# Linear attention beside a GELU MLP: permuted Q features, M in 12 slots, denominators inside an output tile

## The chip, the cores and the metric

The kernel runs on one core of a Trainium2 chip. The metric is the device time of one execution in microseconds (us); the time before is the median of six executions.

## What is computed

One normalised input feeds two blocks, and both are added to the input. Everything is bf16 outside; S = 2048 tokens, D = 640 features, 32 heads of 20 features, F = 1536.

```python
xn = layernorm(x)                      # no weights
q, k, v = split(xn @ wqkv)             # 32 heads of 20 features
pq, pk = phi(q), phi(k)                # phi(t) = (t + 1 if t > 0 else exp(t)) + 1e-6
kv  = einsum("bhsd,bhse->bhde", pk, v)
z   = einsum("bhsd->bhd", pk)          # sum over the tokens
num = einsum("bhqd,bhde->bhqe", pq, kv)
den = einsum("bhqd,bhd->bhq", pq, z) + 1e-6
A   = (num / den) @ wo
B   = gelu(xn @ w1 + b1) @ w2 + b2
out = x + A + B
```

There is no softmax, so K and V are reduced over all tokens before any query is used. The kernel goes one step further: the output of the attention block is (pq / den) @ M, where M, of 640 x 640, is the block-diagonal KV of the heads times wo. Dividing by den is a scaling of pq by head and token.

## The kernel before, in words

Tokens lie in 16 tiles of 128, or 4 chunks of 512. Features lie in 5 tiles of 128 partitions. The order of the work on every engine is the order in which the program issues it; a small planner (`Pl.ins`) notes for every named resource who wrote and who read it last, and puts semaphore waits in front of an instruction for each resource in its `reads` and `writes`. A name that stands for more than what an instruction touches gives a wait that the data doesn't need. The PSUM has 8 banks, handed out in a ring (`take`).

In order on TensorE:

1. Layer norm, its transposed copy, and the MLP's first product with GELU on ACT (`h_unit`, L381). All DMAs of weights are issued by SP in this time, Wo in one and W2 in one.
2. K for 16 tiles (L480). `phi` makes PK from it: exp on ACT (L468), then two VectorE instructions (L469, L471).
3. G = xn' PK for 5 feature tiles (`g_group`, L492). Beside it VectorE adds up PK over the tiles (`z_sums`: L501, then L504 fourteen times, in fp32) and splits the sum into a high and a low bf16 half (L506, L507). GpSimd has nothing to do here but one memset (L487).
4. Q for chunk 0 (`q_chunk`, L529): features of the weight are taken with stride 5, so that feature tile j holds features j, j+5, j+10 and so on: each head has 4 features in every tile, one head to 4 partitions.
5. z, transposed onto partitions by one-column matmuls (`z_step`, L512), and spread by a head mask into ZB (L518).
6. K'V (`kvt_step`, L538): wv' G in 5 blocks of 140 or 160 columns, each masked by VectorE (L542) to keep the heads' own products.
7. Q for chunks 1 to 3.
8. M (`m_step`, L554): 5 feature tiles, each of 16 matmuls with 32 columns of weights (2 halves of the output, 2 source tiles, 4 groups of 32 partitions). Each pair of banks is copied to SBUF by one instruction of ACT (L563) or VectorE (L560); all copies name zsum and zhl, whose place M takes, as written.
9. The denominators (`den_all`, L569), 20 matmuls of 32 columns into one bank. VectorE adds 1e-6 (L573) and takes the reciprocal (L575). `spread` copies each head's row to its 4 partitions with 16 DMAs within SBUF (4 on ACT's queue, 12 on SP's), and `scale_pq` multiplies PQ of a chunk by it, one instruction (L579).
10. The output (`out_mm`, L618): 12 matmuls of W2 and 5 of M for each token tile and half of the columns. The W2 part of the first four tiles is issued ahead of their M part. VectorE adds x and b2 (L594) and the result (L629), SP writes it out.

Of the kernel before, what the change touches and what calls it, by code (L numbers as in the profile page):

```python
# [5 lines left out]
ALU = AluOpType  # L6
ACT = mybir.ActivationFunctionType
P = 128
# [104 lines left out]
def bass_parallel_sum__linear_attn_block__dense_activation_gelu__prompt_kernel(  # L113
# [13 lines left out]
    assert DH == 4 * DT and NC == 4 and P == 4 * H and DT * F >= 2 * (DT + 1) * D  # L127
# [4 lines left out]

    e0 = [DH * ((P * t) // DH) for t in range(DT)]
    e1 = [DH * (-((-(P * (t + 1))) // DH)) for t in range(DT)]
    Wd = [e1[t] - e0[t] for t in range(DT)]

    with contextlib.ExitStack() as es:
# [15 lines left out]
        KVT = W1f[:, DT * D:2 * DT * D].rearrange("p (k d) -> p k d", k=DT)  # L153
        Wqkv = sb("Wqkv", [P, DT, 3 * D], BF16)
        W2 = sb("W2", [P, JT, D], BF16)
        Wo = sb("Wo", [P, DT, D], BF16)
# [9 lines left out]
        hmask = sb("hmask", [P, H], BF16)  # L166
        maskKV = [sb(f"maskKV{t}", [P, Wd[t]], BF16) for t in range(DT)]
# [11 lines left out]
        rsp = sb("rsp", [P, NC, CW], BF16)  # L179
# [14 lines left out]
        def bank(b, lo=0, hi=512):  # L194
            return ps[:, b * 512 + lo: b * 512 + hi]
# [15 lines left out]
        r_Wq, r_Wv, r_W2, r_Wo = R_("Wq"), R_("Wv"), R_("W2"), R_("Wo")  # L211
# [12 lines left out]
        r_KVT = R_("KVT")  # L224
        r_M = [R_("M%d" % j) for j in range(DT)]
        r_zsum, r_zhl, r_z, r_ZB = R_("zsum"), R_("zhl"), R_("z"), R_("ZB")
        r_den, r_rden = R_("den"), R_("rden")
        r_rsp = [[R_("rsp%d_%d" % (c, r)) for r in range(4)] for c in range(NC)]
# [12 lines left out]
        def dma(eng, dst, src, writes, reads=()):  # L241
            Pl.ins(eng, lambda e: e.dma_start(dst, src), reads=reads, writes=writes, dma=True)
# [45 lines left out]
        for t in range(DT):  # L288
            band(maskKV[t][:], r_masks, P * t - e0[t], Wd[t] // DH, DH)
        band(hmask[:], r_hmask, 0, H, 4)  # L290
# [164 lines left out]
        dma("sync", Wo[:], A_wo.rearrange("(k p) n -> p k n", p=P), [r_Wo])  # L455
# [31 lines left out]
        Pl.ins(g, lambda e: e.memset(KVT.bitcast(FP32), 0.0), writes=[r_KVT] + r_W1)  # L487
# [11 lines left out]
        def z_sums():  # L499
            a, c = tord[0], tord[1]  # L500
            Pl.ins(v, lambda e: e.tensor_tensor(out=zsum, in0=PK[:, a, :], in1=PK[:, c, :], op=ALU.add),  # L501
                   reads=[r_PK[a], r_PK[c]], writes=[r_zsum])
            for t in tord[2:]:
                Pl.ins(v, lambda e, t=t: e.tensor_tensor(out=zsum, in0=zsum, in1=PK[:, t, :], op=ALU.add),  # L504
                       reads=[r_PK[t], r_zsum], writes=[r_zsum])
            Pl.ins(v, lambda e: e.tensor_copy(zhl[:, 0, :], zsum), reads=[r_zsum], writes=[r_zhl])  # L506
            Pl.ins(v, lambda e: e.tensor_tensor(out=zhl[:, 1, :], in0=zsum, in1=zhl[:, 0, :], op=ALU.subtract),  # L507
                   reads=[r_zsum, r_zhl], writes=[r_zhl])

        def z_step():  # L510
            b = take(1)
            Pl.ins(pe, [(lambda e, j=j, i=i: e.matmul(bank(b, j, j + 1), zhl[:, i, j:D:DT], onesm[:, 0:1],  # L512
                                                      start=(i == 0), stop=(i == 1)))
                        for j in range(DT) for i in range(2)],
                   reads=[r_zhl, r_ones], writes=[B_[b]])
            Pl.ins(v, lambda e: e.tensor_copy(z_sb[:], bank(b, 0, DT)), reads=[B_[b]], writes=[r_z])
            for j in range(DT):
                Pl.ins(v, lambda e, j=j: e.tensor_scalar(ZB[:, j, :], hmask[:], z_sb[:, j:j + 1], None, ALU.mult),  # L518
                       reads=[r_z, r_hmask], writes=[r_ZB])
# [5 lines left out]
        def q_chunk(c):  # L525
            cc = slice(c * CW, (c + 1) * CW)
            for j in range(DT):
                b = take(1)
                Pl.ins(pe, [(lambda e, k=k, j=j, b=b: e.matmul(  # L529
                    bank(b), Wqkv[:, k, j:D:DT], xnT[:, k, cc],  # L530
                    start=(k == 0), stop=(k == DT - 1))) for k in range(DT)],
                    reads=[r_Wq] + sum(r_xnT[c * CH:(c + 1) * CH], []), writes=[B_[b]])
                phi(bank(b), b, 1, PQ[:, j, cc], r_PQ[c][j], [])

        def kvt_step():
            for t in range(DT):
                b = take(1)
                Pl.ins(pe, [(lambda e, k=k, b=b, t=t: e.matmul(  # L538
                    bank(b, 0, Wd[t]), Wqkv[:, k, 2 * D + t * P:2 * D + (t + 1) * P],
                    GTb[:, k, e0[t]:e1[t]], start=(k == 0), stop=(k == DT - 1))) for k in range(DT)],  # L540
                    reads=[r_Wv] + r_GT, writes=[B_[b]])
                Pl.ins(v, lambda e, b=b, t=t: e.tensor_tensor(  # L542
                    out=KVT[:, t, e0[t]:e1[t]], in0=bank(b, 0, Wd[t]), in1=maskKV[t][:], op=ALU.mult),
                    reads=[B_[b], r_masks], writes=[r_KVT])

        def m_step():
            for j in range(DT):
                b = (0, 2, 4, 0, 2)[j]
                fns = []
                for h in range(2):  # L550
                    for i in range(2):
                        for q in range(4):
                            c0 = j + 32 * DT * q
                            fns.append(lambda e, t=q + i, q=q, i=i, h=h, b=b, c0=c0: e.matmul(  # L554
                                bank(b + h, 0, HW)[32 * q:32 * q + 32, :],
                                KVT[:, t, c0:c0 + 31 * DT + 1:DT], Wo[:, t, h * HW:(h + 1) * HW],
                                start=(i == 0), stop=(i == 1)))
                Pl.ins(pe, fns, reads=[r_KVT, r_Wo], writes=B_[b:b + 2])
                if j in (2, 4):
                    Pl.ins(v, lambda e, b=b, j=j: e.tensor_copy(halves(Msb[:, j, :]), pair(b)),  # L560
                           reads=B_[b:b + 2], writes=[r_M[j], r_zsum, r_zhl])
                else:
                    Pl.ins(s_, lambda e, b=b, j=j: e.activation(halves(Msb[:, j, :]), pair(b), ACT.Copy),  # L563
                           reads=B_[b:b + 2], writes=[r_M[j], r_zsum, r_zhl])

        def den_all():
            b = 6
            for j in range(DT):
                Pl.ins(pe, [(lambda e, j=j, c=c: e.matmul(  # L569
                    bank(b)[H * c:H * c + H, :], ZB[:, j, :], PQ[:, j, c * CW:(c + 1) * CW],  # L570
                    start=(j == 0), stop=(j == DT - 1))) for c in range(NC)],
                    reads=[r_ZB] + [r_PQ[c][j] for c in range(NC)], writes=[B_[b]])
            Pl.ins(v, lambda e: e.tensor_single_scalar(den_sb[:], bank(b), 1e-6, ALU.add),  # L573
                   reads=[B_[b]], writes=[r_den])
            Pl.ins(v, lambda e: e.reciprocal(rden[:], den_sb[:]), reads=[r_den], writes=[r_rden])  # L575

        def scale_pq(c):
            cc = slice(c * CW, (c + 1) * CW)
            Pl.ins(v, lambda e: e.tensor_tensor(  # L579
                out=PQ[:, :, cc], in0=PQ[:, :, cc],  # L580
                in1=rsp[:, c:c + 1, :].broadcast_to((P, DT, CW)), op=ALU.mult),
                reads=r_rsp[c] + r_PQ[c], writes=r_PQ[c])

        def spread(c):
            for r in range(4):
                dma(s_ if c == 0 else "sync", rsp[r:P:4, c, :], rden[H * c:H * c + H, :], [r_rsp[c][r]],
                    reads=[r_rden])
# [14 lines left out]
        ring[0] = 3  # L602
# [3 lines left out]
        m_step()  # L606
        den_all()
        for c in range(NC):
            spread(c)
        scale_pq(0)  # L610

        def out_mm(t, lo, hi, b, w0, w1):
            tok = slice(t * P, (t + 1) * P)
            seq = [(HG[:, jb, tok], W2[:, jb, :], [r_HG[t][jb], r_W2]) for jb in range(JT)]
            seq += [(PQ[:, j, tok], Msb[:, j, :], [r_PQ[t // CH][j], r_M[j]]) for j in range(DT)]
            n = len(seq)
            for i in range(lo, hi):
                Pl.ins(pe, [(lambda e, i=i, x=x, bb=bb: e.matmul(  # L618
                    bank(bb, 0, x[1] - x[0]), seq[i][0], seq[i][1][:, x[0]:x[1]],
                    start=(i == 0), stop=(i == n - 1))) for x, bb in zip(w0, w1)],  # L620
                    reads=seq[i][2], writes=[B_[bb] for bb in w1], mark=(i in (JT - 1, n - 1)))
# [12 lines left out]
        ahead = [4, 0, 2, 6]  # L634
        for t, b in enumerate(ahead):
            out_mm(t, 0, JT, b, HALF, [b, b + 1])
# [6 lines left out]
        ring[0] = 4  # L643
# [7 lines left out]
        t = NT - 1  # L651
        xb(t)
# [49 lines left out]
```

## Time and profile before

| | us |
|---|---|
| median of 6 executions | 209.11 |
| lowest, highest | 208.96, 209.68 |
| the profiled execution | 209.25 |
| its span in the profile | 207.5 |
| busy: TensorE matmul | 202.8 |
| busy: VectorE | 108.7 |
| busy: ACT | 73.9 |
| busy: GpSimd (POOL) | 20.1 |
| between 82.0 and 103.6: TensorE busy | 21.55 |
| between 82.0 and 103.6: VectorE busy | 15.24 |
| between 82.0 and 103.6: GpSimd busy | 0.00 |

The span is what the profiler saw of the profiled execution; the rest of its time lies around it. "Busy" of a matmul runs from its start to its modelled end, and neighbours overlap, so the pace of a stream is read from start times or from the chain, not from the mean duration. A few matmul records are missing from the trace, each of which looks like a hole of one matmul.

### The profile page before, as it was taken

The numbers are of one execution on the slowest core, as the hardware profiler recorded it, in microseconds if no ns is written. First come the engines' busy times: TensorE is split into PE (matmuls) and PEld (weight loads), VectorE is DVE, ScalarE is ACT, GpSimd is POOL, SyncE is SP. The second block draws the span as 40 slices with busy tenths as digits, with TensorE's granted clock in tenths as the row PEclk, the third lists the DMA queues.
The fourth block names the chain that finished last, engine by engine and source line by source line (L and its number), as shares of the span: only waits on it lengthen the run. The fifth ranks groups of instructions, "written<-read, shape, count | busy, mean of one in ns | idle before, by whom it ended". The sixth has DMA issues, their size and how long they took to land.

```text
span 207.5 us, 3961 instructions
## 1 busy us (share of the span) xinstructions
PE 202.8 (98%) x1616; PEld 140.8 (68%) x1622; DVE 108.7 (52%) x213; ACT 73.9 (36%) x146; POOL 20.1 (10%) x57
## 2 busy tenths in 40 slices
PE   7899999999999999999999999999999999999995
PEld 2799887444457777777757556677777777777775
DVE  4788692000008888998068888823853322523322
ACT  2799887666676445111153556100000000000000
POOL 2245447500020000000000000000000000000000
PEclk9999999999999999999999999999999999999999
DMA  5997975999000000000000002941111110010002
GB/s 157 350 279 108 211 108 100 342 319 361 21 0 0 3 0 0 3 0 0 3 0 0 0 2 46 377 140 51 63 66 37 60 35 32 32 35 32 32 33 65
DMA packets 23371, 18.16 MB, mean 88 GB/s; under 512 B 9912, under 2 KB 23352, under 8 KB 23352
## 3 DMA queue, kind: packets, MB, share of 16 engines
q1 hardware_dynamic: 23136, 17.77, 30.5%
q8 instruction: 13, 0.21, 0.4%
q10 hardware_dynamic: 216, 0.13, 0.3%
q14 instruction: 6, 0.05, 0.1%
HBM read 12.62 MB, written 2.62 MB: 73 GB/s over the span
## 4 chain that ended last, share of the span: by engine, by line
PE 96%; DVE 1%; DMA 1%; issue 0%
PE ps L618 36%; PE ps L381 25%; PE ps L492 10%; PE ps L480 10%; PE ps L529 10%; PE ps L554 1%; DMA xPK<-in_A_x_dram 1%; DVE stats L326 1%; PE ps L538 1%; PE ps L569 1%; PE ps L313 0%; PE ps L512 0%; PE ps L298 0%; DVE xn_tm L354 0%; DVE W L659 0%
## 5 line engine op out<-in xcount | busy, mean ns | idle before, releaser
L618 PE MATMUL ps<-W,HG 128*128 128x320 bf16 (+2 forms) x396 | 54.6, 295 | 0.0
L381 PE MATMUL ps<-xnT,W 128*128 128x128 bf16 (+2 forms) x477 | 52.9, 272 | 0.2
L618 PEld LDWEIGHTS ps<-W,HG 128*128 128x128 bf16 x396 | 38.1, 98 | 14.6 <-issue 0.4
L381 PEld LDWEIGHTS ps<-xnT,W 128*128 128x128 bf16 x480 | 36.9, 98 | 15.8 <-issue 0.3
L385 ACT ACTIVATE HG<-ps,b1c 128x128 bf16<-128x128 f32 (+2 forms) x96 | 41.5, 475 | 12.3 <-PE ps L381 10.7
L629 DVE TENSOR_TENSOR W<-ps,xnT 128x640 bf16<-128x640 f32 x15 | 12.4, 825 | 36.9 <-PE ps L618 36.5
L469 DVE TENSOR_SCALAR ek<-ek 128x512 bf16<-128x512 bf16 (+1 forms) x36 | 10.9, 303 | 38.0 <-ACT ek L468 36.8
L468 ACT ACTIVATE ek<-ps 128x512 bf16<-128x512 f32 (+1 forms) x36 | 23.2, 645 | 20.7 <-PE ps L529 11.0
L618 PE MATMUL ps<-Msb,PQ 128*128 128x320 bf16 (+2 forms) x165 | 24.2, 295 | 0.0
L480 PE MATMUL ps<-Wqkv,xnT 128*128 128x320 bf16 x160 | 21.9, 299 | 0.0
L492 PE MATMUL ps<-xPK,xn_tm 128*128 128x320 bf16 x160 | 21.9, 299 | 0.0
L529 PE MATMUL ps<-xnT,Wqkv 128*128 128x512 bf16 x97 | 21.4, 379 | 0.2
L618 PEld LDWEIGHTS ps<-Msb,PQ 128*128 128x128 bf16 x165 | 15.9, 98 | 5.9
L480 PEld LDWEIGHTS ps<-Wqkv,xnT 128*128 128x128 bf16 x160 | 15.7, 98 | 6.2
L492 PEld LDWEIGHTS ps<-xPK,xn_tm 128*128 128x128 bf16 x160 | 15.7, 98 | 6.1
L529 PEld LDWEIGHTS ps<-xnT,Wqkv 128*128 128x128 bf16 x100 | 11.7, 118 | 9.5
L326 DVE BATCH_NORM_STATS2 stats<-xPK 128x6 f32<-128x320 bf16 x32 | 15.1, 473 | 3.8 <-DMA xPK<-in_A_x_dram 3.3
L471 DVE SCALAR_TENSOR_TENSOR PQ<-ps,ek 128x512 bf16<-128x512 f32 x20 | 13.8, 691 | 2.1
L471 DVE SCALAR_TENSOR_TENSOR xPK<-ps,ek 128x640 bf16<-128x640 f32 x16 | 13.2, 825 | 1.7
L504 DVE TENSOR_TENSOR Msb<-Msb,xPK 128x640 f32<-128x640 f32 x14 | 11.6, 825 | 0.5
L496 ACT ACTIVATE W<-ps 128x640 bf16<-128x640 f32 x5 | 3.5, 704 | 18.2 <-PE ps L492 18.2
L354 DVE TENSOR_SCALAR xn_tm<-xPK,aggr,rstd 128x640 bf16<-128x640 bf16 (+2 forms) x17 | 7.3, 434 | 2.7 <-POOL rstd L342 1.5
(57 smaller groups left out, 76.5 us busy)
## 6 DMA issues: line engine op xcount, KB each, us to landing
xnT<-in_A_x_dram SPq DMA_DIRECT2D x4, 640.0 KB, 6.4
Wqkv<-in_A_wqkv_dram SPq DMA_DIRECT2D x3, 800.0 KB, 6.7
out_dram<-W SPq DMA_DIRECT2D x15, 160.0 KB, 1.8
W<-in_B_w_dram SPq DMA_DIRECT2D x4, 480.0 KB, 5.9
W<-in_B_w_dram SPq DMA_DIRECT2D x1, 1920.0 KB, 16.1
xPK<-in_A_x_dram SPq DMA_DIRECT2D x2, 640.0 KB, 7.0
Wo<-in_A_wo_dram SPq DMA_DIRECT2D x1, 800.0 KB, 10.5
xPK<-in_A_x_dram SPq DMA_DIRECT2D x4, 160.0 KB, 3.8
```

Source lines behind the costliest of these rows:

```text
L326: Pl.ins(v, lambda e: e.bn_stats(stats[:, s, 6 * h:6 * h + 6], x_in[:, t, h * HW:(h + 1) * HW]), reads=r_x[t], writes=[r_stats[s]])
L381: Pl.ins(pe, [(lambda e, k=k: e.matmul(bank(b, 0, w), W1[:, k, jb * P:(jb + 1) * P], xnT[:, k, tok], start=(k == 0), stop=(k == DT - 1))) ...
L385: Pl.ins(s_, lambda e: e.activation(HG[:, jb, tok], bank(b, 0, w), ACT.Gelu_apprx_tanh, bias=b1c[:, jb:jb + 1]), reads=[B_[b], r_b1c], wri ...
L468: Pl.ins(s_, lambda e: e.activation(e2, src, ACT.Exp), reads=br, writes=[r_ek[s]])
L469: Pl.ins(v, lambda e: e.tensor_scalar(et, et, 1.0, 1e-6, ALU.min, ALU.add), reads=[r_ek[s]], writes=[r_ek[s]])
L471: Pl.ins(v, lambda e: e.scalar_tensor_tensor(out=d2, in0=src, scalar=0.0, in1=e2, op0=ALU.max, op1=ALU.add), reads=br + [r_ek[s]], writes= ...
L480: fns.append(lambda e, k=k, h=h, b=b, t=t: e.matmul(bank(b + h, 0, HW), xnT[:, k, t * P:(t + 1) * P], Wqkv[:, k, D + h * HW:D + (h + 1) * ...
L492: Pl.ins(pe, [(lambda e, t=t, h=h, b=b, f=f, i=i: e.matmul(bank(b + h, 0, HW), xn_tm[:, t, f * P:(f + 1) * P], PK[:, t, h * HW:(h + 1) * H ...
L504: Pl.ins(v, lambda e, t=t: e.tensor_tensor(out=zsum, in0=zsum, in1=PK[:, t, :], op=ALU.add), reads=[r_PK[t], r_zsum], writes=[r_zsum])
L529: Pl.ins(pe, [(lambda e, k=k, j=j, b=b: e.matmul(bank(b), Wqkv[:, k, j:D:DT], xnT[:, k, cc], start=(k == 0), stop=(k == DT - 1))) for k in ...
L618: Pl.ins(pe, [(lambda e, i=i, x=x, bb=bb: e.matmul(bank(bb, 0, x[1] - x[0]), seq[i][0], seq[i][1][:, x[0]:x[1]], start=(i == 0), stop=(i = ...
L629: Pl.ins(v, lambda e: e.tensor_tensor(out=halves(out_sb[:, s, :]), in0=pair(b), in1=halves(x_res[:, t, :]), op=ALU.add), reads=B_[b:b + 2] ...
```

## The change

The order of Q's features is changed. Of a head's 20 features, 8 go to feature tile 0 or 1 (heads 0 to 15) or to tile 2 or 3 (heads 16 to 31) in each of the two, and 4 to tile 4. The columns of wq are copied into that order by 25 GpSimd instructions, into the place of wk, once K is done; the sum z and K'V are put in the same order. Then:

- Wo is loaded as 8 overlapping slots of 128 rows, one for each 4 heads, and K'V is computed in 8 blocks of 80 columns into two banks, masked by three VectorE instructions and split into three pieces (KVP) by four GpSimd copies.
- For feature tiles 0 to 3 of M, 4 matmuls give one half of the output; for tile 4 it is 8: 48 in all.
- Each bank of M is copied by itself, the left half of the columns by ACT and the right half by VectorE, and each has its own name in the planner; zsum and zhl are no longer named as written.
- The order around M is: the left half of tile 0's W2 product, the denominators in the other bank of that pair, M (with the addition of 1e-6 after its second feature tile), the reciprocal and the spreads, the right half of tile 0's W2 product, and tiles 1 to 3.
- A spread is three DMAs of 128 rows for each chunk, all on ACT's queue, with a repeated source; the scaling of a chunk is three instructions.

```diff
-        Wo = sb("Wo", [P, DT, D], BF16)
+        Wo = sb("Wo", [P, NW, D], BF16)
...
-        dma("sync", Wo[:], A_wo.rearrange("(k p) n -> p k n", p=P), [r_Wo])
+        for w in range(NW):
+            dma("sync", Wo[:, w, :], A_wo[E0[w]:E0[w] + P, :], [r_Wo[w]])
...
-        Pl.ins(g, lambda e: e.memset(KVT.bitcast(FP32), 0.0), writes=[r_KVT] + r_W1)
+        def parts(ap, i):
+            v4 = ap.rearrange("p (h t) -> p h t", t=DH)
+            if i == DT - 1:
+                return v4[:, :, 2 * TA:DH]
+            return v4[:, HH * (i // 2):HH * (i // 2) + HH, TA * (i % 2):TA * (i % 2) + TA]
+
+        def plain(ap, i):
+            return ap[:, i * P:(i + 1) * P].rearrange("p (h t) -> p h t", t=TB if i == DT - 1 else TA)
+
+        Pl.ins(g, lambda e: e.memset(KVP[2], 0.0), writes=[r_KVP[2]] + r_W1)
+        for k in range(DT):
+            for i in range(DT):
+                Pl.ins(g, lambda e, k=k, i=i: e.tensor_copy(plain(Wqkv[:, k, D:2 * D], i), parts(Wqkv[:, k, 0:D], i)),
+                       reads=[r_Wq], writes=[r_Wk, r_WqP])
...
-            Pl.ins(v, lambda e: e.tensor_copy(zhl[:, 0, :], zsum), reads=[r_zsum], writes=[r_zhl])
...
+            for i in range(DT):
+                Pl.ins(v, lambda e, i=i: e.tensor_copy(plain(zhl[:, 0, :], i), parts(zsum, i)),
+                       reads=[r_zsum], writes=[r_zhl])
...
-                    bank(b), Wqkv[:, k, j:D:DT], xnT[:, k, cc],
+                    bank(b), Wqkv[:, k, D + j * P:D + (j + 1) * P], xnT[:, k, cc],
                     start=(k == 0), stop=(k == DT - 1))) for k in range(DT)],
-                    reads=[r_Wq] + sum(r_xnT[c * CH:(c + 1) * CH], []), writes=[B_[b]])
+                    reads=[r_WqP] + sum(r_xnT[c * CH:(c + 1) * CH], []), writes=[B_[b]])
...
+                Pl.ins(pe, [(lambda e, k=k, b=b, w=w: e.matmul(
+                    bank(b, (w % 4) * WD, (w % 4) * WD + WD), Wqkv[:, k, 2 * D + E0[w]:2 * D + E0[w] + P],
+                    GTb[:, k, w * WD:(w + 1) * WD], start=(k == 0), stop=(k == DT - 1)))
+                    for w in ws for k in range(DT)],
                     reads=[r_Wv] + r_GT, writes=[B_[b]])
...
+        def m_copy(j, b, h):
+            cols = slice(h * HW, (h + 1) * HW)
+            if h == 0:
+                Pl.ins(s_, lambda e: e.activation(Msb[:, j, cols], bank(b + h, 0, HW), ACT.Copy),
+                       reads=[B_[b + h]], writes=[r_M[j][h]])
+            else:
+                Pl.ins(v, lambda e: e.tensor_copy(Msb[:, j, cols], bank(b + h, 0, HW)),
+                       reads=[B_[b + h]], writes=[r_M[j][h]])
+
+        def m_step(js, bs, after):
+            for n, (j, b) in enumerate(zip(js, bs)):
                 for h in range(2):
-                    for i in range(2):
+                    fns, reads = [], []
+                    for a in range(2 if j == DT - 1 else 1):
                         for q in range(4):
...
+                    Pl.ins(pe, fns, reads=reads, writes=[B_[b + h]])
+                    m_copy(j, b, h)
+                if n == 1:
+                    after()
...
-            for r in range(4):
-                dma(s_ if c == 0 else "sync", rsp[r:P:4, c, :], rden[H * c:H * c + H, :], [r_rsp[c][r]],
+            for r, (h, n) in enumerate(((0, HH), (HH, HH), (0, H))):
+                src = rdv[H * c + h:H * c + h + n].broadcast_to((n, P // n, CW))
+                dma(s_, rsp[:, c, r, :], src, [r_rsp[c][r]] + (sum(r_xn, []) if c + r == 0 else []),
                     reads=[r_rden])
...
-        ahead = [4, 0, 2, 6]
-        for t, b in enumerate(ahead):
+        out_mm(0, 0, JT, b0, HALF[:1], [b0])
+        den_mm(b0 + 1)
+        m_step([0, 1, DT - 1, 2, 3], ahead[1:] + ahead[1:3], lambda: den_eps(b0 + 1))
+        den_rec()
+        for c in range(NC):
+            spread(c)
+        scale_pq(0)
+        out_mm(0, 0, JT, b0, HALF[1:], [b0 + 1])
+        for t in range(1, 4):
+            b = ahead[t]
             out_mm(t, 0, JT, b, HALF, [b, b + 1])
```

## The prediction

> **What bounds the kernel now.** I read the page first: busy shares, then the chain that ended last.
>
> ```profile
> PE 202.8 (98%) x1616; PEld 140.8 (68%) x1622; DVE 108.7 (52%) x213; ACT 73.9 (36%) x146; POOL 20.1 (10%) x57
> ...
> PE 96%; DVE 1%; DMA 1%; issue 0%
> ```
>
> TensorE is the chain for 96% of the span, at full clock in all 40 slices. So only two things count: matmul time taken out of its stream, and holes that other engines put into it. The chain in order of time, around the change:
>
> ```profile
> 99.88 3.67 PE ps L492 x27
> 103.55 0.05 issue
> 103.60 5.34 PE ps L529 x24
> 108.94 0.36 PE ps L512 x10
> 109.31 1.58 PE ps L538 x25
> ...
> 127.08 3.03 PE ps L554 x80
> 130.11 1.08 PE ps L569 x20
> 131.19 3.91 PE ps L618 x28
> ```
>
> Columns: start, length, what. L538 is K'V, L554 is M, L569 the denominators, L618 the output products. There is no hole at 103.6 (a record of one 0.216 us matmul is missing there), and from M to the first W2 product TensorE spends 131.19 - 127.08 = 4.11 us. Then the waits, and the other engines on the timeline:
>
> ```profile
> PEld ps L554 <- ACT Msb L563: 0.3, 1, 0.3
> DVE PQ L579 <- DMA rsp<-rden: 4.6, 1, 4.6
> ```
> ```profile
> 83.76 0.81 DVE L501 TENSOR_TENSOR Msb<-xPK 128x640 f32<-128x640 bf16 x1
> 84.61 12.00 DVE L504 TENSOR_TENSOR Msb<-Msb,xPK 128x640 f32<-128x640 f32 x14
> 96.65 0.49 DVE L506 CAST Msb<-Msb 128x640 bf16<-128x640 f32 x1
> 97.17 0.83 DVE L507 TENSOR_TENSOR Msb<-Msb 128x640 bf16<-128x640 f32 x1
> ...
> 131.13 0.82 DVE L560 CAST Msb<-ps 128x640 bf16<-128x640 f32 x1 [0.90 <-ACT Msb L563]
> 131.87 0.68 DVE L573 TENSOR_SCALAR den_sb<-ps 128x512 f32<-128x512 f32 x1
> 132.59 3.35 DVE L575 RECIPROCAL rden<-den_sb 128x512 bf16<-128x512 f32 x1
> 140.54 1.49 DVE L579 TENSOR_TENSOR PQ<-PQ,rsp 128x2560 bf16<-128x2560 bf16 x1 [4.60 <-DMA rsp<-rden]
> ```
>
> M waits once for its own copies. The reciprocal, spread and scaling end at 142.0; TensorE first needs scaled PQ at 144.2, so they have 2.1 us to spare.
>
> **What the Trainium skill says.**
> 1. "SBUF — State Buffer", Who interferes with whom: GpSimd's SBUF ports are VectorE's second pair, taken as an exclusive lock; a VectorE instruction with two SBUF inputs, or in a two-port mode, and a GpSimd instruction that reads SBUF block each other. The trace has one such overlap and agrees. A VectorE normalisation ran from 32.91 to 33.36:
>
> ```profile
> 33.03 0.53 POOL L280 TENSOR_SCALAR_AFFINE_SELECT maskKV<-maskKV 128x140 bf16<-128x140 bf16 x1
> 33.64 0.34 POOL L284 TENSOR_SCALAR_AFFINE_SELECT maskKV<-maskKV 128x140 bf16<-128x140 bf16 x1
> ...
> 38.57 0.42 POOL L280 TENSOR_SCALAR_AFFINE_SELECT hmask<-hmask 128x32 bf16<-128x32 bf16 x1
> ```
>
> The select beside it took 0.53 us, the same one alone 0.34: 0.19 longer, so it got the port about 0.13 us before VectorE's recorded end.
> 2. "TensorEngine Tiling (Array Packing)", Key Properties: changing the tiling mode drains TensorE. The trace agrees: the start times of single matmuls leave 0.09 us extra before the first 32-column matmul and 0.10 after the last.
> 3. "TensorE: Matmul & The Clock Gate", Back-to-back issue gap: columns / 2.4 + 2.5 ns. The trace's 140-column matmuls come every 60 to 61 ns, as that gives.
>
> **The change, part by part.**
>
> *M.* Before: 80 matmuls of 32 columns, in 20 groups of four that start together, 0.136 us apart: 2.72, plus 0.15 waiting for a bank and 2 x 0.03 of group starts, 2.93 us. Denominators 5 x 0.216 = 1.08, drain 0.10: 4.11, as the chain says. After: 48 matmuls, 12 groups, 1.63 + 0.03. With 1.08 and 0.10: 2.85. **Gain 1.27.** The 12 W2 matmuls of tile 0's first half only move ahead of it (12 x 0.136 = 1.63 either way); the number of mode changes stays. They also cover the last phi of chunk 3, which ends at 128.92, while the denominators' last group now starts near 129.6.
>
> *The denominator bank.* Tile 0's second half writes the bank in which the denominators stood, so it now waits for the addition of 1e-6 (VectorE), queued behind two M copies. With chunk 3's matmuls over at 126.92: W2 half to 128.55, drain to 128.64, denominators to 129.72, M to 131.38. A copy sees its product 0.35 us after the group's start (ACT started 0.35 after j=0's last group). A half copy costs: VectorE 0.82 - 320 x 1.09 ns = 0.47 (slope from 0.82 at 640 and 0.68 at 512), next one 0.08 sooner as its rows show; ACT 0.70 - 320 x 0.83 ns = 0.43. VectorE: copies at 130.24 and 130.64, addition 131.04 to 131.72, seen at 131.77. TensorE would be ready at 131.49. **Stall 0.3** (0 to 0.7). By the same sums the M products that reuse a bank find it free: j=2 at 130.84 against 130.54, j=3 at 131.11 against about 131.05. The copies no longer wait for each other through the zsum/zhl names (the 0.90 wait shown); before, that cost only VectorE.
>
> *K'V.* 25 matmuls took 1.58. After: 40 of 80 columns. Price 80/2.4 + 2.5 = 36 ns; the one-column matmuls of L512 with full weight loads came 40 ns apart, so 36 to 40: 1.44 to 1.60. Value -0.05; if a weight load bound at 56 ns, the pace of 128-column matmuls, +0.66. Its masks (three VectorE instructions of about 1.1 us, not five of 1.95) come earlier. The four small GpSimd copies into KVP follow by 117 at the latest; M needs them at 129.7.
>
> *Permuted Q weights.* 25 GpSimd copies of 128x128, after the last K matmul (82.0) and before chunk 0 of Q (103.6): they write where Wk lay, and chunk 0 waits for all 25. Nothing in the trace shows a GpSimd copy. Bounds: not below the 128x128 memset's 0.205, not above the select with 32 short rows, 0.42; I take 0.30 (the 128x128 select took 0.29), plus 0.07 hand-over between dependent GpSimd instructions. Free of VectorE: 25 x 0.37 = 9.3, done at 91.3. But zsum runs from 83.76 with two SBUF inputs each. Four copies before it; then copy and sum alternate at 0.70 (0.83 less the 0.13 above) + 0.30 = 1.0: 15 sums to 98.8, 19 copies done; the other six alternate with the short zhl pieces at about 0.5: 101.8. **Cost 0, with 1.8 us to spare.** The zhl pieces (ten instead of two, about 3.1 us instead of 1.35) also end some 5 us later than 98, near 103; the first phi needs VectorE at 105.3 and z at 108.8. The Q matmuls keep 512 columns at 0.216.
>
> *Reciprocal, spread, scaling.* VectorE does three more half copies after the addition (0.40 apart), so the reciprocal starts at about 133.0 and ends 136.3; 13 wait instructions at 0.06 each (SP's pace) stand ahead of the first spread; three DMAs of 128 rows instead of four of 32, issued at 0.6 each, landing 1.9 to 2.6 after issue: 141. Scaling in three pieces (0.69 + 0.69 + 0.42, from 1.49 for 2560), the first ones while the last lands: 141.5. TensorE needs it at 131.8 + 7 x 12 x 0.136 = 143.2. **Hidden, 1.7 us to spare.** All 12 spreads move from SP to ACT, behind which nothing waits; SP's outputs lose their queue-mates. The later scalings cost VectorE 0.3 more each, at 40% load. Eight Wo DMAs instead of one delay W2's issue by some 3 us to 41; it landed in 16 and is needed at 126.9.
>
> *Sum.* -1.27 + 0.3 - 0.05 = -1.0. The profiled execution took 209.25 with a span of 207.5; so 208.2 and 206.5. It lies 0.14 above the median of 209.11: **208.1**.
>
> **Rivals.**
> A. *The forecast*, 207.8 to 208.5.
> B. *The full saving without the bank stall*: VectorE's addition is early enough. 209.1 - 1.3 = 207.75.
> C. *Copies bind M.* VectorE's five half copies and the addition are 2.7 us of work beside 1.66 of M; if each is slower by 0.15, TensorE waits about 0.7 more: 208.8. For: M's copies are halves with a fixed part each. Against: three bank pairs.
> D. *GpSimd is late at 103.6: slower.* Place: chunk 0's first matmul. Price: the lateness, one for one. It decides when 25 copies take more than 103.6 + 1.0 + 0.4 - 82.0 = 23 us, 0.92 each. With 0.45 a copy: 3 before zsum, 15 beside it at 1.15 to 101.0, 7 at 0.65 to 105.6: 2.0 late, 210.1. Shut out entirely until zhl ends at 99.9: 21 x 0.37 more, 107.7, 4.1 late, 212.2. For: zsum keeps the port 80% of 14 us. Against: the lock passes on at each instruction's end, and the estimate has 1.8 us left.
> E. *The spread is late.* 128-row DMAs with a repeated source are not in the trace. Over 1.7 us late it costs TensorE the rest: 208.5 to 209.5.
>
> **Chances.** A 0.44, B 0.08, C 0.13 (half of it under 208.7), D 0.27 (0.04 still faster, 0.06 about even, 0.17 slower), E 0.08 (0.02 faster, 0.02 even, 0.04 slower). About 0.2% (0.42 us) is what a measurement of this kernel can tell from no change. Faster by more than that: 0.44 + 0.08 + 0.06 + 0.04 + 0.02 = 0.64; within it 0.07 + 0.06 + 0.02 = 0.15; slower 0.17 + 0.04 = 0.21. The range goes from just under B, 207.6, to 209.9: some 0.11 of D lies above it, little below. The likeliest case's own range is A's.
>
> **What would show it.** Right: the row of M with 48 matmuls in about 1.7 us; TensorE's wait for the addition of 1e-6 near 131.5 of 0.2 to 0.4; no wait of the first Q matmul on GpSimd; GpSimd's last Wqkv copy ending by 103. Wrong: a wait of TensorE on GpSimd at 103.6 (D), waits on ACT's or VectorE's M copies between 130 and 133 (C), or on VectorE's PQ scaling at 143 (E); K'V at over 2 us.

## The result, and the profile after

| | before | after |
|---|---|---|
| median, us | 209.62 (208.95 to 211.43, 58 runs) | 208.39 (207.82 to 210.3, 27 runs) |
| ratio, 95% interval | 1 | 0.9936 (0.9918 to 0.9954) |
| profiled execution, us | 209.25 | 208.84 |
| its span | 207.5 | 207.1 |
| first recorded matmul of Q's chunk 0 to the start of VectorE's last instruction, us | 101.67 | 100.42 |

The change makes the kernel faster by 0.64% (0.46 to 0.82%); the medians differ by 1.23 us. 208.1 and a change of 1.0 had been forecast. The median of before, 209.11 in six runs, was 209.62 in 58: single executions of one kernel lie up to 2.5 us apart. In the traces of the kernels below, Q's chunk 0 begins anywhere between 103.4 and 105.4 (but for the kernel with 50 copies, which holds it back), though nothing ahead of it on TensorE was changed. So the traces are compared by the last row of the table, which leaves that part out: in it the gain is 1.25 us. (The very first matmul of chunk 0 has no record in either trace, nor in most of those below; the row counts from the second.)

The page of the kernel after, with the group of GpSimd copies that is new in it (busy time, mean ns, idle time before it):

```profile
PE 201.7 (97%) x1599; PEld 137.5 (66%) x1605; DVE 111.6 (54%) x230; ACT 73.7 (36%) x148; POOL 34.0 (16%) x83
...
L509 POOL COPY Wqkv<-Wqkv 128x128 bf16<-128x128 bf16 x25 | 15.1, 603 | 22.9 <-PE ps L490 21.4
```

GpSimd has 14 us more to do, and the end of the program doesn't see it. The chain in order of time (start, length, what; L539 is z, L566 K'V, L610 M, L620 the denominators, L673 the output products, and its first row here is tile 0's left half):

```profile
104.11 5.34 PE ps L556 x24
109.45 0.23 PE ps L539 x10
109.68 1.46 PE ps L566 x40
...
127.33 1.63 PE ps L673 x12
128.96 1.19 PE ps L620 x20
130.15 0.30 PE ps L610 x8
...
130.47 0.89 DVE Msb L595 x2
131.36 0.61 DVE den_sb L626
...
132.02 72.49 PE ps L673 x549
...
204.53 0.29 DVE W L722
```

The last row of the chain of before is

```profile
205.27 0.29 DVE W L659
```

The terms are best read from start times, because a piece of the chain can begin at the modelled end of a matmul or at the start of the next one. TensorE's rows of before in the timeline (start, length, engine and line, count):

```profile
108.78 0.52 PE L512 MATMUL ps<-onesm,Msb 128*128 128x1 bf16 x10
109.17 1.72 PE L538 MATMUL ps<-W,Wqkv 128*128 128x140 bf16 x25
110.94 16.14 PE L529 MATMUL ps<-xnT,Wqkv 128*128 128x512 bf16 x73
...
131.12 13.21 PE L618 MATMUL ps<-W,HG 128*128 128x320 bf16 x96
```

From the first z matmul to chunk 1 of Q it is 110.94 - 108.78 = 2.16 before and 111.19 - 109.29 = 1.90 after (rows below): -0.26 for z and K'V, of which the chain gives 0.13 to z (0.36 to 0.23) and 0.12 to K'V (1.58 to 1.46). From there to the W2 product that follows M and the denominators it is 131.12 - 110.94 = 20.18 before; after, less the 1.63 us of W2 that only moved ahead, 132.02 - 111.19 - 1.63 = 19.20: -0.98. Together -1.24, where the stretch gave -1.25. Ahead of the rows above, at 20.98, the chain has a hole of 0.45 us, long before any changed instruction of TensorE. The trace of before has none there; more on it below.

The chain leaves TensorE at 130.45 and comes back at 132.02 through two copies of M and the addition of 1e-6: that is the one new wait. TensorE's own rows and VectorE's, from the timeline of after (in brackets the idle time before and what ended it):

```profile
85.12 12.00 DVE L527 TENSOR_TENSOR Msb<-Msb,xPK 128x640 f32<-128x640 f32 x14
...
109.29 0.39 PE L539 MATMUL ps<-onesm,Msb 128*128 128x1 bf16 x10
...
111.19 16.14 PE L556 MATMUL ps<-xnT,Wqkv 128*128 128x512 bf16 x73
127.16 1.79 PE L673 MATMUL ps<-W,HG 128*128 128x320 bf16 x12
...
129.97 1.80 PE L610 MATMUL ps<-Wo,W 128*32 128x320 bf16 x48
132.02 11.58 PE L673 MATMUL ps<-W,HG 128*128 128x320 bf16 x84 [0.24 <-DVE den_sb L626]
143.44 5.60 PE L673 MATMUL ps<-Msb,PQ 128*128 128x320 bf16 x40
...
131.28 0.68 DVE L626 TENSOR_SCALAR den_sb<-ps 128x512 f32<-128x512 f32 x1
...
141.03 1.03 DVE L635 TENSOR_TENSOR PQ<-PQ,xn_tm 128x1024 bf16<-128x1024 bf16 x2 [0.78 <-DMA xn_tm<-rden]
```

M is 48 matmuls in 1.8 us (80 in 3.1 before), and TensorE waits for the addition: 0.24 us after the modelled end of M, 0.31 by start times (worked out below). The reciprocal ran from 133.07 for 3.34 us; the last row is the end of the scaling of chunk 0, done at 142.06, 1.4 us before the first product of PQ and M.

### The profile page after: what moved, and what is told of

It reads as the page before. It is cut to its first block, busy times and chain, and to the rows that moved or that the text cites. A ratio compares the mean times of both kernels' runs of the same rounds, so it can differ in the third digit from the quotient of the medians.

```text
span 207.1 us, 3983 instructions
## 1 busy us (share of the span) xinstructions
PE 201.7 (97%) x1599; PEld 137.5 (66%) x1605; DVE 111.6 (54%) x230; ACT 73.7 (36%) x148; POOL 34.0 (16%) x83
## 3 DMA queue, kind: packets, MB, share of 16 engines
q10 hardware_dynamic: 1752, 1.58, 4.4%
## 4 chain that ended last, share of the span: by engine, by line
PE 95%; DVE 2%; DMA 1%; issue 1%
PE ps L673 36%; PE ps L390 25%; PE ps L515 10%; PE ps L490 10%; PE ps L556 10%; DMA xPK<-in_A_x_dram 1%; DVE stats L335 1%; PE ps L566 1%; PE ps L620 1%; DVE Msb L595 0%; PE ps L322 0%; DVE den_sb L626 0%; PE ps L307 0%; PE ps L610 0%; DVE W L722 0%
## 5 line engine op out<-in xcount | busy, mean ns | idle before, releaser
L673 PE MATMUL ps<-W,HG 128*128 128x320 bf16 (+2 forms) x396 | 54.8, 295 | 0.2 <-DVE den_sb L626 0.2
L673 PEld LDWEIGHTS ps<-W,HG 128*128 128x128 bf16 x396 | 38.1, 98 | 14.8 <-DVE den_sb L626 0.5
L673 PE MATMUL ps<-Msb,PQ 128*128 128x320 bf16 (+2 forms) x165 | 24.2, 295 | 0.0
L673 PEld LDWEIGHTS ps<-Msb,PQ 128*128 128x128 bf16 x165 | 15.9, 98 | 5.9
L509 POOL COPY Wqkv<-Wqkv 128x128 bf16<-128x128 bf16 x25 | 15.1, 603 | 22.9 <-PE ps L490 21.4
L556 PEld LDWEIGHTS ps<-xnT,Wqkv 128*128 128x128 bf16 x100 | 9.7, 98 | 11.4
```

Source lines behind the costliest of these rows:

```text
L509: Pl.ins(g, lambda e, k=k, i=i: e.tensor_copy(plain(Wqkv[:, k, D:2 * D], i), parts(Wqkv[:, k, 0:D], i)), reads=[r_Wq], writes=[r_Wk, r_WqP])
L556: Pl.ins(pe, [(lambda e, k=k, j=j, b=b: e.matmul(bank(b), Wqkv[:, k, D + j * P:D + (j + 1) * P], xnT[:, k, cc], start=(k == 0), stop=(k == ...
L673: Pl.ins(pe, [(lambda e, i=i, x=x, bb=bb: e.matmul(bank(bb, 0, x[1] - x[0]), seq[i][0], seq[i][1][:, x[0]:x[1]], start=(i == 0), stop=(i = ...
```

## The experiments

In the table the last column is the stretch from the first recorded matmul of Q's chunk 0 to the start of VectorE's last instruction, in the profiled execution of each. Each ratio is to executions of before made beside that kernel, whose medians were 209.62, 209.75 and 209.72. Unless said otherwise, a kernel is an edit of the kernel after.

| kernel | median us (range, runs) | ratio to before, 95% | stretch, us |
|---|---|---|---|
| before | 209.62 (208.95 to 211.43, 58) | 1 | 101.67 |
| after | 208.39 (207.82 to 210.3, 27) | 0.9936 (0.9918 to 0.9954) | 100.42 |
| the same again | 208.46 (207.85 to 210.3, 22) | 0.9942 (0.9918 to 0.9966) | 100.42 |
| W2 half split | 208.09 (207.85 to 209.59, 7) | 0.9935 (0.9900 to 0.9970) | 100.11 |
| false waits back | 209.67 (209.15 to 211.54, 14) | 1.0003 (0.9978 to 1.0028) | 101.64 |
| M twice | 209.45 (209.19 to 211.76, 22) | 0.9995 (0.9970 to 1.0019) | 101.75 |
| M copied by pairs | 209.09 (208.24 to 211.59, 20) | 0.9983 (0.9958 to 1.0007) | 100.69 |
| order of before | 209.15 (208.74 to 211.29, 20) | 0.9970 (0.9945 to 0.9995) | 101.30 |
| before, without its false waits | 209.57 (208.88 to 211.25, 20) | 1.0001 (0.9976 to 1.0026) | 101.49 |
| 50 copies on GpSimd | 215.59 (214.35 to 216.12, 4) | 1.0252 (1.0195 to 1.0309) | not used |
| few sums | 208.64 (one run) | one run only | not used |

### The kernel after, once more

No edit: it shows how far the stretch can be trusted.

> The changed kernel once more, beside the kernels that it is compared with. Theory (TensorE's stream got shorter by eight groups of M, z and K'V, and a new wait of 0.3 us for the addition of 1e-6 gives some of it back): 1.2 to 1.3 us under the kernel before. Rival (the saving is scatter of the start, where this kernel's profile has a hole of 0.45 us and the other has none): within 0.4 us of the kernel before.

The median came again within 0.1 us, and the stretch was 100.42 both times, in an execution whose chunk 0 began 0.1 us later. So differences of 0.1 us in the stretch are read here, on the strength of this one repetition; in the medians, with 20 runs each, the interval is 0.5 us wide to either side.

### M's products doubled: what is a group of M worth on TensorE?

```diff
-                    Pl.ins(pe, fns, reads=reads, writes=[B_[b + h]])
+                    Pl.ins(pe, fns + fns, reads=reads, writes=[B_[b + h]])
```

The second pass computes the same values over again.

> Every matmul of M is issued twice (the second overwrites or repeats the first; tile 4 of M comes out the same), so M has 24 groups of four instead of 12, with the same copies. Theory (M is paid one for one in TensorE's stream, 0.136 us a group): 12 x 0.136 = 1.63 us more, less the 0.3 of the wait for the addition, which the longer M hides: 1.3 us slower than the changed kernel. Rival (the copies bind M): under 0.5 us slower.

The chain of it:

```profile
129.48 3.26 PE ps L610 x96
132.74 72.43 PE ps L673 x549
```

The stretch grew by 1.33. 96 products took exactly twice the 1.63 us of 12 groups, without a wait among them, and the wait for the addition is gone from the chain, since TensorE now comes 1.6 us later: 1.63 - 0.31 = 1.32 was due, 1.33 came. A group of M costs TensorE 0.136 us one for one. The copies have twice as long for each bank here; that they keep up at the full pace is seen in the kernel after, whose 48 products run without a wait.

### The wait for the addition taken out: three W2 products held back

```diff
-        out_mm(0, 0, JT, b0, HALF[:1], [b0])
+        out_mm(0, 0, 9, b0, HALF[:1], [b0])
         den_mm(b0 + 1)
...
         scale_pq(0)
+        out_mm(0, 9, JT, b0, HALF[:1], [b0])
         out_mm(0, 0, JT, b0, HALF[1:], [b0 + 1])
```

Three of the 12 W2 products (0.41 us) come after M instead of ahead of the denominators; they fill the wait.

> Only the place of three of tile 0's left W2 matmuls changes: nine stand ahead of the denominators, three after M. Theory: they fill the 0.31 us in which TensorE waits for the addition of 1e-6, and the last phi (done 0.2 us ahead of need) still comes in time; TensorE has no idle time between M and W2 but the drain of 0.1, and the time falls by 0.3 us against the changed kernel. Rival (the wait is not for the addition but for M's last copies or the change of the tiling mode): the hole stays, 0 us.

TensorE goes from M straight to W2; in the chain there is no detour over VectorE. The stretch is shorter by 0.31. The same is read from start times: M's last group and the W2 product behind it, first in after, then in this kernel:

```profile
131.47 0.31 PE L610 MATMUL ps<-Wo,W 128*32 128x320 bf16 x4
132.02 0.31 PE L673 MATMUL ps<-W,HG 128*128 128x320 bf16 x1 [0.24 <-DVE den_sb L626]
```
```profile
130.92 0.31 PE L610 MATMUL ps<-Wo,W 128*32 128x320 bf16 x4
131.16 0.31 PE L673 MATMUL ps<-W,HG 128*128 128x320 bf16 x1
```

0.55 us from one to the other with the wait, 0.24 without: 0.31. The change of the tiling mode is in both, so it is not the cause. The bank stall was real and cost what the forecast gave for it, and rival B (no stall) was wrong for the kernel as it was changed. In the medians it gives 208.09 against 208.39, which the runs can't tell apart; by the trace it is the best version found here.

### The false waits put back

```diff
-                       reads=[B_[b + h]], writes=[r_M[j][h]])
+                       reads=[B_[b + h]], writes=[r_M[j][h], r_zsum, r_zhl])
```

In both branches of the copy: each copy of half of M names zsum and zhl again, so it waits for the one before it on the other engine.

> The changed kernel with zsum and zhl named again as written by every copy of M, so that ten half copies on two engines go one after the other. Theory: 0.5 us each in a row, so the addition of 1e-6 ends at 133.0 and not 132.0, and TensorE's second half of tile 0 starts 1.0 us later: 0.8 to 1.5 us slower than the changed kernel. Rival (as in the kernel before, such waits cost VectorE alone): 0 us.

The timeline of it, the last group of M and the W2 products behind it (M's first group was at 131.28):

```profile
133.85 0.32 PE L610 MATMUL ps<-Wo,W 128*32 128x320 bf16 x4 [0.28 <-DVE Msb L595]
134.45 11.68 PE L673 MATMUL ps<-W,HG 128*128 128x320 bf16 x84 [0.28 <-DVE den_sb L626]
```

and its waits, the two engines for each other (us in all, times, longest):

```profile
DVE Msb L595 <- ACT Msb L592: 3.7, 4, 1.8
ACT Msb L592 <- DVE Msb L595: 2.1, 3, 0.7
```

The stretch is 1.22 longer, nearly the whole gain of the change: ACT and VectorE take turns instead of working side by side, so M's banks and the addition come too late. (Its chunk 0 began 1.3 us later, which the stretch leaves out. That was lost before 13.5 us, where no changed instruction stands: the first 15 matmuls of the MLP took 1.60 us there and 1.00 in after.)

### The same edit the other way, in the kernel before

```diff
-                           reads=B_[b:b + 2], writes=[r_M[j], r_zsum, r_zhl])
+                           reads=B_[b:b + 2], writes=[r_M[j]])
```

> The kernel before, without zsum and zhl as written by the copies of M; nothing else. Theory: VectorE's addition and reciprocal start 0.5 us earlier, in front of slack of 2.1 us: no change of the time (within 0.1 us). Rival (the false waits are part of what the change gained): 0.3 us or more faster than the kernel before.

M's row in the timeline of the kernel before:

```profile
127.01 3.10 PE L554 MATMUL ps<-Wo,W 128*32 128x320 bf16 x80
```

and without the false waits:

```profile
126.96 2.92 PE L554 MATMUL ps<-Wo,W 128*32 128x320 bf16 x80
```

The stretch is 0.18 shorter, more than the 0.1 expected, and M's row shows all of it: 2.92 for 3.10. ACT's second copy had waited for its first one through a name (0.80 us from start to start; the two took 1.50 together, and 1.30 without the false wait), and held the banks that the last feature tile of M was to write. By the traces, removing the false waits alone was worth 0.2 us in the old arrangement; the medians, 209.57 and 209.72, can't tell. They cost 1.2 in the new one. The likely reason is that M now fills its banks in 1.63 us, not 2.92, through twice as many copies; no run tries these two apart.

### M copied by whole pairs, one engine each

```diff
-                    m_copy(j, b, h)
+                m_pair(n, j, b)
```

`m_pair` copies both halves with one instruction, ACT for the even and VectorE for the odd ones, as before the change.

> The changed kernel, but M is copied by pairs of banks, tile by tile, one instruction of ACT or VectorE in turn, as in the kernel before, without false waits. Theory: VectorE's copy of the second tile takes 0.82 instead of two halves of 0.40, so the addition of 1e-6 ends 0.25 us later and TensorE's wait grows from 0.3 to 0.55: 0.2 to 0.3 us slower than the changed kernel. Rival (copies bind M): 0.7 us or more slower.

The detour in its chain, as it stood at 130.47 in that of after (L603 is VectorE's copy, L634 the addition; the last Q matmul ended at 127.11):

```profile
130.60 0.82 DVE Msb L603
131.42 0.61 DVE den_sb L634
```

The stretch is 0.27 longer. The detour over VectorE explains it. VectorE's first copy can start only when both halves of a pair are there, 3.49 us after the last Q matmul (130.60 - 127.11) instead of 3.14 (130.47 - 127.33), and it is one of 0.82 us with the addition queued behind it. So the addition begins 4.23 us after the last Q matmul, and in after 3.95 (131.28 - 127.33): 0.28 later, the whole difference. Copying by halves is worth some 0.3 us. (The medians differ by 0.7, which their interval of 0.5 to either side does not set apart from 0.3.)

### M and the denominators in the old order, in banks of their own

```diff
-        out_mm(0, 0, JT, b0, HALF[:1], [b0])
-        den_mm(b0 + 1)
-        m_step([0, 1, DT - 1, 2, 3], ahead[1:] + ahead[1:3], lambda: den_eps(b0 + 1))
+        ahead = [(b0 + d) % 8 for d in (4, 0, 2, 6)]
+        m_step([0, 1, DT - 1, 2, 3], [b0, (b0 + 2) % 8, (b0 + 4) % 8, b0, (b0 + 2) % 8], lambda: None)
+        den_mm((b0 + 7) % 8)
+        den_eps((b0 + 7) % 8)
...
-        out_mm(0, 0, JT, b0, HALF[1:], [b0 + 1])
-        for t in range(1, 4):
+        for t in range(4):
```

All W2 products come after, so nothing stands between chunk 3 of Q and M.

> The changed kernel, but M stands straight after Q's chunk 3, then the denominators, then all W2 products, as in the kernel before. Theory: M's right halves can be copied only when VectorE is through with the last phi, 2.0 us after Q's last matmul, so the two tiles that reuse a bank wait, and Q's end to W2's start takes 4.4 us instead of 3.1: 1.3 us slower than the changed kernel, about the kernel before. Rival (twelve slots alone bring the saving, the order brings nothing): within 0.3 us of the changed kernel.

The timeline, the last 12 matmuls of M and VectorE:

```profile
129.39 0.72 PE L610 MATMUL ps<-Wo,W 128*32 128x320 bf16 x12 [0.80 <-DVE Msb L595]
...
128.24 0.69 DVE L481 SCALAR_TENSOR_TENSOR PQ<-ps,ek 128x512 bf16<-128x512 f32 x1
128.85 2.07 DVE L595 CAST Msb<-ps 128x320 bf16<-128x320 f32 x5
```

The stretch is 0.88 longer, where 1.3 was expected: the size was missed, because VectorE made its five copies back to back, 0.40 apart, once it was free. The place is as thought. VectorE is busy with the last phi of chunk 3 and starts its first copy at 128.85; before that it can't empty a bank of M, so TensorE waits 0.80 us in the middle; M began at 127.11 and the W2 products at 131.12, 4.01 us later, where the kernel before took 4.11. With the order of before, most of what 32 fewer matmuls save would be lost again in that wait; the 1.63 us of W2 products ahead of M are what hides the phi.

### Twice the copies on GpSimd: where does the cover end?

```diff
-                Pl.ins(g, ...)
+                for _ in range(2):
+                    Pl.ins(g, ...)
```

Each of the 25 copies of wq is issued twice.

> The changed kernel with each of the 25 GpSimd copies of the Q weights made twice. Theory (a copy takes 0.36 with its hand-over alone and 0.86 beside a zsum addition, and chunk 0 waits for the last): 5 to 84.4, 15 beside zsum to 97.4, 30 alone to 108.1; TensorE waits 4.0 us at 104.1: 3.5 to 4.5 us slower than the changed kernel, and VectorE's sums take 12.0 us as before. Rival (no copy bound the start of chunk 0, or VectorE loses the time): under 1 us, or zsum longer than 13 us.

TensorE in the timeline (L510 and L557 are the lines 509 and 556 of after); GpSimd's 50 copies ran until 107.73:

```profile
108.19 4.01 PE L557 MATMUL ps<-xnT,Wqkv 128*128 128x512 bf16 x11 [4.33 <-POOL Wqkv L510]
```

The record has TensorE without a matmul for 4.33 us. The first of chunk 0's 25 matmuls has no record here either; it must have run in the last 0.4 us of that gap, at the pace of those that follow it, so TensorE waited some 3.9 us by this estimate (4.0 expected). So chunk 0 does depend on these copies. The kernel lost more than the wait: the 24 recorded matmuls took 6.82 instead of 5.34. Two windows from the end of that wait on (length, busy times of five engines, then the granted clock, DMA share, GB/s), show why:

```profile
107.75:111.16 3.41, 2.97 (x7) 1.16 (x9) 0.29 (x1) 0.60 (x1) 0.00 (x0) 0.50 0.02 5
111.16:115.01 3.85, 3.85 (x25) 1.83 (x24) 2.96 (x7) 1.79 (x3) 0.00 (x0) 1.00 0.00 0
```

The clock is at half for 3.41 us, in which seven recorded matmuls take 2.97 us, 0.42 each instead of 0.216. Half of 3.41 is 1.7 us lost, and 3.9 + 1.7 = 5.6: the spans of the two profiled executions, 212.6 and 207.1, differ by 5.5. Rival D's price, the lateness one for one, holds for the wait itself but leaves out this loss. The Trainium skill, "TensorE: Matmul & The Clock Gate", Part 1: The HAM clock gate, says that an idle window of about 3.4 us halves TensorE's clock until it has been busy for about as long. This trace agrees.

The medians differ by 7.2 us (215.59 and 208.39), well over the 3.5 to 4.5 that were expected. Two of the four executions had a mean granted clock of 0.984 instead of 0.992, which by the same working is another 1.7 us; none of these was profiled, so what is left between 5.5 and 7.2 stays open.

### Few sums beside the copies: what made them slow?

In the kernel after, nearly every copy took either about 0.3 or about 0.8 us. That line's own view there (least, median and longest duration in ns):

```profile
L509 POOL COPY Wqkv<-Wqkv x25: 291/797/884, 82.5 to 98.8; 128x128 bf16<-128x128 bf16 x25
```

The edit leaves out 13 of the 14 in-place additions of zsum (and so computes another z), so that VectorE has little to do there:

```diff
-            for t in tord[2:]:
+            for t in tord[2:3]:
```

> Leaves out 13 of the 15 additions of a feature group that VectorE makes for the normalising sum (its value is then wrong), so that VectorE is idle over most of the stretch in which GpSimd makes its 25 copies. Theory (a copy on GpSimd of 0.30 us takes 0.80 only because it alternates with VectorE's two-input sums): all copies but the two or three beside the remaining sums and casts take 0.30 each, 0.36 from start to start, and the last ends near 92 us instead of 99.1. Rival (these copies are slow in that stretch for another reason, such as the DMA or ScalarE traffic): still 0.80 each, end near 99. Both: the time is unchanged within 0.2 us, since K'V waits for neither.

The same view of the edited kernel:

```profile
L509 POOL COPY Wqkv<-Wqkv x25: 291/296/882, 82.6 to 92.3; 128x128 bf16<-128x128 bf16 x25
```

The median fell from 797 to 296 ns, and all 25 were done at 92.6 (82.56 + 10.05 in its timeline) instead of 99.1. VectorE's additions were the cause, and not other traffic of that stretch. The time was 208.64 in its single run, within the scatter of after.

## Why the prediction was right, point by point

*The mechanism and the size of M.* 12 groups at 0.136 us: forecast 1.63 + 0.03, measured 131.47 - 129.97 + 0.136 = 1.64, from the first start to the last group's and one spacing more, and 3.26 when doubled. Denominators 5 x 0.216 and the drain of 0.10 held too: 1.19 for both in the chain.

*The bank stall.* Forecast 0.3, measured 0.31, by start times and when taken out. The addition was forecast to begin at 131.04 with chunk 3's matmuls over at 126.92. They were over at 127.16, where the first W2 product starts; 0.24 later puts the addition at 131.28, and it began at 131.28. Together with M: -1.27 + 0.3 = -0.97 forecast, -0.98 measured.

*Two terms were too small.* z was given nothing and brought 0.13: its one-column matmuls came 40 ns apart in the kernel before and 25 ns after, with weights that are now contiguous instead of taken with stride 5 (a load of them took 131 ns before and 96 after, in the median). K'V was given 0.05 of a bracket from -0.14 to +0.66 and brought 0.12: 40 matmuls at 36 ns, which is the price that was named, and which the spacing cited in the prediction gives for 80 columns. The 40 ns of the one-column matmuls had been carried over to K'V as its upper figure; they belonged to the strided weights. These two, 0.13 and 0.07, are the difference between the 1.02 of the sum and the 1.25 measured, but for 0.03. No run changes the stride alone; that the stride is the cause is argued from the two kernels.

*GpSimd had more to spare than thought.* Copies alone took 0.296 (0.30 forecast). Beside the sums the forecast let copy and sum alternate at 0.70 + 0.30 = 1.0. They went one copy to one sum, but at 12.00 / 14 = 0.857, VectorE's own pace: the 14 sums took 12.00 us in both kernels. The 25 copies were done at 99.1, not 101.8, 5.0 us ahead of chunk 0's first record and not 1.8, and the zhl pieces ended at 100.5, not at 103. The step that failed is the addition of the two durations; the copy's time is inside the sum's recorded 0.857, not on top of it. Here the Trainium skill, "SBUF — State Buffer", Who interferes with whom, has the rule (an exclusive lock of VectorE's second pair of ports against GpSimd, who blocks being a matter of order), and the trace agrees for GpSimd: 0.797 for 0.296, and back when the sums were gone. It shows no loss for VectorE on these sums. The short subtractions of zhl got only a little slower: 0.323 in the median in the kernel with few sums, where GpSimd copies all the while, and 0.293 in the kernel after, where the copies are nearly over.

*One sentence was wrong.* Of the false waits it says "before, that cost only VectorE". They cost TensorE 0.18 us in the kernel before, and 1.22 in the new arrangement. The sum is not touched, since the 0.15 us of waiting for a bank was taken out of M's old time as another term; its cause had not been found.

*The rivals.* B is out (the stall was there, 0.31 by the split). C, that copies bind M, didn't happen: the 48 products ran without a wait among them. But it is what happened in the old order (0.80 of waiting) and with the false waits; two parts of the change are there to keep it away. D decides where it was said to, but with 5.0 us to spare it is out; had it come with the 4.1 us of its worst case, its price would likely have been too low by the clock that such a wait costs (1.7 us on 3.9). E: the last of chunk 0's spreads was scaled at 142.06, TensorE came at 143.44, so 1.4 us were left of the 1.7 forecast (the spreads took 3.3 us from issue to landing in the median, not the 1.9 to 2.6 of the forecast, but were issued earlier).

*What was luck.* The absolute time was forecast as 208.1 from a median of before that turned out 0.5 us too low, and the gain was 0.2 larger than forecast. The two errors go against each other: 209.62 less the forecast gain would be 208.6, outside the likeliest range of 207.8 to 208.5.

*What stays open.* In the trace of after TensorE has a hole of 0.45 us near 21 us, in a repetition 0.48, with the W2 half split 0.36, with M copied by pairs 0.21, in the old order 0.11, with few sums 0.44, with 50 copies 0.25, in the four other traces (before, before without its false waits, M twice, the false waits put back) under 0.1. It comes before any changed instruction of TensorE runs. What the diff changes by then is the loading of the weights (eight DMAs for Wo); M twice has the same loading and no hole, so this is not shown to be the cause. It was not tried by itself. The stretch leaves the hole out; the medians, which hold it, differ by 1.23.

## What to carry to other kernels

On an engine that is busy for 98% of the time, count the groups of matmuls that a change removes and multiply by their spacing: with the stall, that term was right to 0.01 us here. Then ask of every bank in the neighbourhood who empties it and what that engine has in its queue at that moment; order, copies by halves and honest names were worth 0.9, 0.3 and 1.2 us here, each undone alone, beside a gain of 1.25 in all, though none of them removes any work. Waits between two engines that cost little at one pace (0.18 us) can eat the gain when the producer becomes faster.

## What the runs showed of the hardware

- A GpSimd copy of 128x128 bf16 within SBUF takes 0.296 us alone, 0.80 beside VectorE additions with both inputs in SBUF (one copy for each addition), and those additions lose nothing: 14 in 12.00 us with and without the copies.
- One-column matmuls came 25 ns apart with contiguous weights, which is the floor that the Trainium skill states in "TensorE: Matmul & The Clock Gate", Wait — 56ns, not 53.3ns?, and 40 ns apart with weights of stride 5 (two kernels; the stride was not changed by itself).
- After some 3.9 us without a matmul TensorE ran at half its clock for 3.41 us, which cost 1.7 us on top of the wait (one trace; where between no wait and 3.9 us this begins was not tried).
